# Sigmoid attention with a top-1 mixture of experts: gate products as bfloat16 parts, scatters and value loads moved

## The chip, the cores and the metric

The kernel runs on one core of a Trainium2 chip. The metric is the device time of one execution in microseconds (us). A profile of one execution stands beside three timed runs; engines are named as the profile names them: PE (TensorE matmul), PEld (its weight loads), DVE (VectorE), ACT (ScalarE), POOL (GpSimd) and SP (SyncE, which here only issues DMAs).

## The reference

Attention with a sigmoid in place of the softmax, over 8 batches, 12 heads, 448 positions and head size 64, gives a row of 768 numbers for each of 3584 tokens. Then each token goes to the one of 8 experts with the largest logit:

```python
scores = scale * np.matmul(q, k.transpose(0, 1, 3, 2)) - np.log(S)
x = np.matmul(1.0 / (1.0 + np.exp(-scores)), v)      # tokens x 768 after a transpose
logits = x @ w_gate
e = argmax(logits);  gate = softmax(logits)[e]
out[token] = gate * (relu(x @ w1[e]) @ w2[e])        # w1: 768x1024, w2: 1024x768
```

## The kernel before

**Attention.** A batch of 448 tokens is a block, 12 heads are 6 pairs of heads, and two pairs together are a unit of `ST` = 7 steps, one for each chunk of 64 key positions. A step `s` issues four score products (L612, recorded as 8 instructions), two sigmoids on ACT (L599), and the four products with the values of step `s - 2` (L627). `PB` = 21 steps are one block. Within a stretch of 21 steps a step is named below by its place r, 0 to 20. At the end of a unit ACT and DVE copy the sums out of PSUM (L635, L636) and DVE transposes them for a token-major copy in DRAM (L464), which SP writes (L472). Queries and keys arrive transposed in 32x32 blocks (`load_pair`, L519, eight DMAs for a pair) and DVE turns them (`turn`, L582). Values arrive by `load_values` (L526 for an even pair, one DMA; L570 for an odd one, two DMAs). The two PSUM tiles of a unit come from one of two pools; two following units that use the same pool share its two tiles.

**Routing.** For each block `gate_a` to `gate_d` compute the logits, the expert of each token, its gate, and where its record (row, gate) goes in a DRAM list `recs`; `put_records` scatters the records by four indirect DMAs on POOL (L417). The tiles `si` and `rec` that a scatter reads exist once.

**Dense stage.** A block's tokens are then all run through the expert that most of them chose (`moe`): 8 sums for the hidden layer of 18 products each (L249), then 6 sums of 24 (L268), 288 products in all, each operand split into a high and a low part. A product is one `yield`; a tick of the interleaving is 14 of them. The results are multiplied by the gates in a second layout, `gate_rows`: `gate_m` (L433) spreads the block's gates over 14 columns, and `gate_e` (L440, L442) brings them to the right partitions by four float32 products with the 0/1 matrix `place`, into a PSUM tile of the attention's pool, which DVE copies. Both are issued in the ticks 5 and 6 of the stage, those of the last block in ticks 8 and 9 of the stage before.

**Skipped stages.** For the blocks 1 to 5 (`LEFT`) the dense stage stands in an `If` on the flag that over 240 tokens chose the expert; the branch stands behind step r = 1 of the stretch two blocks later. Otherwise the `Else` only loads and turns what the steps to come need, and attention goes on. In this data one of the five, block 4, takes the `Else`. Its tokens, and those of the other experts, are run at the end from the records, gathered by row.

**Order.** The program's order on each engine is written out by hand under `tc.manual_schedule()`: dictionaries say at which step or tick a load, a turn or a gate step is issued (`LATER`, `LAST`, `BETWEEN`, `BESIDE_GATES`, `LATE_GATES`). Each DMA queue (SP's, POOL's) is in order. The letters in the `GATES` tables are the gate steps, "p" the scatter, "m" and "e" the two gate steps of the dense stage, "x" the token-major writes.

Of the kernel before, what the change touches and what calls it, by code (L numbers as in the profile page):

```python
# [25 lines left out]
def tile_sigmoid_attention_top1_moe(  # L26
# [86 lines left out]
    HR = 16  # L113
    place = const.tile([P, P + HR], F32, name="place")
    spot = const.tile([CP, NCH, NB], F32, name="spot")

    def places():

        aside = opool.tile([P, 512], F32, tag="ob", name="aside")
        halves = aside[:, : 2 * HR].rearrange("p (h r) -> p h r", h=2)  # L120
        nc.vector.tensor_reduce(
            halves, ident.rearrange("p (i h r) -> p h r i", i=4, h=2), axis=AX.X, op=ALU.add
        )
        for h in range(2):
            to = place.rearrange("p (n r) -> p n r", r=HR)[:, h::2]
            nc.vector.tensor_copy(to, halves[:, h].unsqueeze(1).broadcast_to([P, 5 - h, HR]))
        off = aside[:CP, P : P + NCH * NB].rearrange("p (c j) -> p c j", c=NCH)
        nc.gpsimd.iota(
            off, pattern=[[CP, NCH], [-32, NB]], base=0, channel_multiplier=1, allow_small_or_imprecise_dtypes=True
        )  # L130
        nc.vector.tensor_scalar(spot, off, 0.0, None, op0=ALU.is_ge)
        nc.vector.scalar_tensor_tensor(spot, off, 32.0, spot, op0=ALU.is_lt, op1=ALU.mult)

# [99 lines left out]
    def moe(b, wts):  # L233
# [7 lines left out]
        for j in range(KF):  # L241
# [3 lines left out]
            for t in range(KD):  # L245
                xh, xl = xch[b, t]
                ws = slice(t * P, (t + 1) * P)
                for n, (a, b_) in enumerate(((whi, xh), (whi, xl), (wlo, xh))):
                    nc.tensor.matmul(ps[:, :S], a[:, ws], b_, start=(t == 0 and n == 0), stop=(t == KD - 1 and n == 2))  # L249
                    yield  # L250
            if j % 2 == 0:
                two = [hpool.tile([P, 1024], F32R, tag=f"h{x}{j}", name=f"h{x}_{b}_{j}") for x in "hl"]
# [177 lines left out]
    def gate_m(b):  # L430

        gm[b] = small.tile([CP, NCH, NB], F32, tag="gm", name=f"gm_{b}")
        nc.vector.tensor_tensor(gm[b], spot, gates[:CP, b].unsqueeze(2).broadcast_to([CP, NCH, NB]), op=ALU.mult)  # L433

    def gate_e(b):

        pg = small_ps(b, "pg")
        by_place = gm.pop(b)
        for c in range(NCH):
            nc.tensor.matmul(pg[:, :NB], place[:CP, c % 2 * HR : c % 2 * HR + P], by_place[:, c], start=(c == 0), stop=(c == NCH - 1))  # L440
        gate_rows[b] = small.tile([P, NB], F32, tag="gt", bufs=2, name=f"gt_{b}")
        nc.vector.tensor_copy(gate_rows[b], pg[:, :NB])  # L442

# [172 lines left out]
    def weighted(s):  # L616
# [40 lines left out]
        0: lambda u: turn(2 * u + 2, "k"),  # L657
        1: lambda u: (turn(2 * u + 2, "q"), load_values(2 * u + 2)),
        3: lambda u: turn(2 * u + 3, "k"),
        4: lambda u: (turn(2 * u + 3, "q"), load_values(2 * u + 3)),  # L660
    }
# [38 lines left out]
    def attention():  # L700

        order = ExitStack()
        order.enter_context(tc.manual_schedule())
        for g in range(2):
# [16 lines left out]
        def gate_step(b, what):  # L721
# [13 lines left out]
            elif what == "m":  # L735
                gate_m(b)
            elif what == "e":
                gate_e(b)
            elif what == "x":
# [9 lines left out]
        BESIDE_GATES = {  # L749
            0: "xa", 1: "b", 3: "c", 4: "l", 6: "d", 7: "p", 8: "m", 9: "e", 11: (0,), 12: (1,), 13: (2,),  # L750
        }
# [3 lines left out]
        LATE_GATES = {  # L755
            2: "a", 4: "b", 6: (0, "c"), 7: (1,), 8: (2, "l"), 11: "d", 16: "p",
        }
        ALONE = 2 * PB

        for s in range(N_ST + 2):  # L760
# [25 lines left out]
            for what in LATE_GATES.get(r, ()) if late else ():  # L786
                gate_step(nb, what)
            if i in (1, 5) and not ALONE - ST < s < ALONE + 2 or s == ALONE - 5:
                gate_step(None, "x")
# [10 lines left out]
            if b in LEFT:  # L800
# [10 lines left out]
                with tc.If(whole >= 1, label=f"whole_{b}") as whole_if, tc.manual_schedule():  # L811
                    for tick in range(14):
                        if tick in (5, 6):
                            gate_step(b, "me"[tick - 5])
                        if tick == 0:
# [6 lines left out]
                with whole_if.Else(), tc.manual_schedule():  # L822
# [4 lines left out]
                    load_values(2 * u + 3)  # L827
                    load_pair(2 * u + 4)
                    for at in rows:
                        token_rows(*at)  # L830
                    load_pair(2 * u + 5)
                    for g in (6, 7):
                        load_pair(2 * u + g, nc.gpsimd)
                continue
            for tick in range(0 if b else 1, 20 if b < B - 2 else 15):
                yield TICK
                for what in (BESIDE_GATES if b else FIRST_GATES).get(tick, ()):
                    gate_step(b + 1, what)
                if tick in (5, 6):
                    gate_step(b, "me"[tick - 5])  # L840
                if b == 0 and tick == 2:
                    put_records(0)
                todo = BETWEEN if b else FIRST_BETWEEN
# [4 lines left out]
            if b == 0:  # L848
                for n in range(2):
                    scores(ALONE + n)  # L850
        order.close()

# [17 lines left out]
    def until(n):  # L870
        more(left - n)

    for n in attention():
        more(n)
    att.close()


    order = ExitStack()
    order.enter_context(tc.manual_schedule())
    rest = ctx.enter_context(tc.tile_pool(name="rest", bufs=1))  # L880
# [335 lines left out]
```

## Time and profile before

| | us |
|---|---|
| three timed runs: median (lowest to highest) | 787.92 (785.06 to 789.79) |
| the profiled execution: its own time | 788.64 |
| the profiled execution: its span | 786.9 |
| PE busy | 772.8 (98%), granted clock 0.994 of full speed |
| DVE busy, ACT busy, POOL busy | 439.3, 374.7, 140.9 |
| gate products L440: 56 instructions, busy | 6.7 |

Busy time on PE is that of pipelined instructions, so a busy stretch is compared by the starts of its instructions. Times in the rows are us from the start of the span.

### The profile page before, as it was taken

The page shows a single profiled execution, that of the slowest core. Times are in us where ns is not written, and L with a number is a line of the kernel's source. Part 1 is how long each engine was busy: PE and PEld are TensorE (multiplying, and loading weights), DVE is VectorE, ACT ScalarE, POOL GpSimd, SP SyncE. Part 2 cuts the span into 40 slices and gives each one's busy share as a digit, 9 for nine tenths or more (in the row PEclk, how much of TensorE's full clock was granted, in tenths as well). Part 3 has the DMA queues.
Part 4 walks back from the last instruction along what each step waited for, and adds up shares of the span by engine and source line. Part 5 has one row for each costly group of instructions (what it writes and reads, how often), then busy time and mean ns, then how long its engine had stood idle before and what let it go on. Part 6 is the DMA issues. An engine that isn't in the chain of part 4 may idle for free. (4 is left out here: it accounts for less than half of the span.)

```text
span 786.9 us, 15431 instructions
## 1 busy us (share of the span) xinstructions
PE 772.8 (98%) x5536; PEld 592.3 (75%) x5536; DVE 439.3 (56%) x944; ACT 374.7 (48%) x681; POOL 140.9 (18%) x217
## 2 busy tenths in 40 slices
PE   9999999999999999999999969999999999999996
PEld 5545899789974699647996424799648998999885
DVE  3465767335437754376443837654376574476763
ACT  5876432863217632284323838532383321435662
POOL 4433204100021001210012151001220232031011
PEclk9999999999999999999999989999999999999999
DMA  8968789557524984268932586981266356599111
GB/s 170 187 131 219 177 199 222 106 113 189 105 53 101 237 208 95 48 145 216 213 58 46 79 178 149 238 197 24 47 161 176 101 130 173 185 295 320 53 36 38
DMA packets 268147, 114.45 MB, mean 145 GB/s; under 512 B 192380, under 2 KB 257932, under 8 KB 268062
## 3 DMA queue, kind: packets, MB, share of 16 engines
q1 hardware_dynamic: 258766, 91.82, 48.9%
q0 software_dynamic: 8864, 20.87, 11.1%
q8 instruction: 46, 0.75, 0.4%
q10 hardware_dynamic: 432, 0.69, 0.3%
q14 instruction: 39, 0.32, 0.2%
HBM read 94.30 MB, written 22.38 MB: 148 GB/s over the span
## 5 line engine op out<-in xcount | busy, mean ns | idle before, releaser
L599 ACT ACTIVATE at<-sc,bias_s 128x448 f32<-128x448 f32 x336 | 195.2, 634 | 127.1 <-PE sc L612 125.7
L627 PE MATMUL av<-at,vn 64*64 64x448 f32 x1344 | 184.1, 538 | 5.9 <-DMA vn<-in_v_dram 4.9
L612 PE MATMUL sc<-qt,kt 64*64 64x448 f32 x1344 | 184.6, 545 | 0.2 <-PEq L811 0.2
L612 PEld LDWEIGHTS sc<-qt,kt 64*64 64x64 f32 x1344 | 83.2, 189 | 58.6 <-issue 41.3
L249 PE MATMUL ps<-xh,w1h 128*128 128x448 f32 x336 | 124.4, 370 | 0.0
L249 PE MATMUL ps<-xh,w1l 128*128 128x448 f32 x336 | 123.7, 368 | 0.0
L268 PE MATMUL ps<-hh,w2h 128*128 128x448 f32 x336 | 123.0, 366 | 0.0
L249 PE MATMUL ps<-xl,w1h 128*128 128x448 f32 x336 | 123.0, 366 | 0.0
L268 PE MATMUL ps<-hh,w2l 128*128 128x448 f32 x336 | 123.0, 366 | 0.0
L268 PE MATMUL ps<-hl,w2h 128*128 128x448 f32 x336 | 122.8, 365 | 0.0
L284 POOL DMA_DIRECT2D out_dram<-ob x84 | 53.8, 647 | 359.6 <-DVE ob L279 353.8
L627 PEld LDWEIGHTS av<-at,vn 64*64 64x64 f32 x1344 | 63.7, 133 | 65.3 <-issue 61.3
L254 ACT ACTIVATE hh<-ps 128x448 fp32r<-128x448 f32 x56 | 30.5, 545 | 145.3 <-PE ps L249 145.3
L177 ACT CAST w2h<-wst 128x512 fp32r<-128x512 f32 x84 | 54.1, 662 | 81.1 <-PE ps L268 79.4
L178 DVE TENSOR_TENSOR w2l<-wst,w2h 128x512 fp32r<-128x512 f32 x84 | 56.7, 688 | 54.1 <-ACT w2h L177 52.2
L255 DVE SCALAR_TENSOR_TENSOR hl<-ps,hh 128x448 fp32r<-128x448 f32 x56 | 34.9, 622 | 76.2 <-ACT hh L254 76.1
L249 PEld LDWEIGHTS ps<-xh,w1h 128*128 128x128 f32 x336 | 63.1, 188 | 9.0 <-issue 3.5
L249 PEld LDWEIGHTS ps<-xh,w1l 128*128 128x128 f32 x336 | 63.1, 188 | 6.8 <-issue 1.1
L249 PEld LDWEIGHTS ps<-xl,w1h 128*128 128x128 f32 x336 | 63.1, 188 | 5.8 <-issue 0.4
L268 PEld LDWEIGHTS ps<-hh,w2h 128*128 128x128 f32 x336 | 63.1, 188 | 5.1 <-issue 0.2
L268 PEld LDWEIGHTS ps<-hl,w2h 128*128 128x128 f32 x336 | 63.1, 188 | 4.9
L268 PEld LDWEIGHTS ps<-hh,w2l 128*128 128x128 f32 x336 | 63.1, 188 | 4.9
(154 smaller groups left out, 821.7 us busy)
## 6 DMA issues: line engine op xcount, KB each, us to landing
wst<-in_moe_w_dram SPq DMA_DIRECT2D x50, 512.0 KB, 3.9
wst<-in_moe_w_dram SPq DMA_DIRECT2D x56, 384.0 KB, 5.3
x_tok<-xt SPq DMA_DIRECT2D x64, 168.0 KB, 2.8
kn<-in_k_dram SPq DMA_DIRECT2D x176, 56.0 KB, 3.7
out_dram<-ob POOLq DMA_DIRECT2D x84, 112.0 KB, 3.0
qn<-in_q_dram SPq DMA_DIRECT2D x160, 56.0 KB, 2.9
kept<-in_moe_w_dram SPq DMA_DIRECT2D x12, 512.0 KB, 9.5
vn<-in_v_dram SPq DMA_DIRECT2D x16, 224.0 KB, 4.9
```

What stands on the lines that cost most here:

```text
L177: (nc.vector.tensor_copy if early else nc.scalar.copy)(hi, st)
L178: eng.tensor_tensor(lo, st, hi.bitcast(F32), op=ALU.subtract)
L249: nc.tensor.matmul(ps[:, :S], a[:, ws], b_, start=(t == 0 and n == 0), stop=(t == KD - 1 and n == 2))
L254: nc.scalar.activation(hh[:, :S], ps[:, :S], AF.Relu)
L255: nc.vector.scalar_tensor_tensor(hl[:, :S], ps[:, :S], 0.0, hh[:, :S].bitcast(F32), op0=ALU.max, op1=ALU.subtract)
L268: nc.tensor.matmul(ps[:, :S], a, b_, start=(j == 0 and n == 0), stop=(j == KF - 1 and n == 2))
L284: nc.gpsimd.dma_start(out[b * S : (b + 1) * S, cols].rearrange("(j r) f -> r j f", r=32), obv[32 * i : 32 * (i + 1)])
L599: nc.scalar.activation(at, ps[:, :S], AF.Sigmoid, bias=bias_s, scale=SCALE)
L612: nc.tensor.matmul(ps[quarter(g, h), :S], ks, ops[g, "q"][OWN[h]], start=True, stop=True)
L627: nc.tensor.matmul(psv[g][OWN[h], :S], ops[g, "v"][rows, c, :], at[rows], start=(c == 0), stop=(c == KC - 1))
```

## The change

- The gates are split by DVE into three bfloat16 parts whose sum is the float32 gate (`gate_m`: four small operations ahead of the product, which grows from 56 to 168 columns), `place` and `spot` become bfloat16, and the four float32 products become two bfloat16 products of 42 columns.
- These two products are issued behind the last product of the sixth hidden sum (j = 5), into the 64 columns of that PSUM bank that the sum leaves free; a DVE reduction adds the three parts in place of the copy. Step "e" goes from the tables, "m" stays at tick 5 (tick 8 for the last block).
- The scatter of a late stretch, issued at r = 16, is issued at r = 10 of the next late stretch, just ahead of the gate step "d" of r = 11; the last such one at tick 2 of the stage of block 6.
- In `LATER` the values of both pairs of the next unit are loaded in step 1; those of the odd pair were loaded in step 4.
- In the `Else` the second pair's loads go from SP to POOL and the third pair's from POOL to SP.
- The scope of the manual order is opened ahead of the attention and stays open into the last section.

```diff
-    place = const.tile([P, P + HR], F32, name="place")
-    spot = const.tile([CP, NCH, NB], F32, name="spot")
+    HB = NB // 2
+    place = const.tile([P, P + HR], BF16, name="place")
+    spot = const.tile([CP, NCH, HB], BF16, name="spot")
...
+            if j == 5:
+                gate_e(b, ps[:, S : S + 3 * NB])
...
     def gate_m(b):
-        gm[b] = small.tile([CP, NCH, NB], F32, tag="gm", name=f"gm_{b}")
-        nc.vector.tensor_tensor(gm[b], spot, gates[:CP, b].unsqueeze(2).broadcast_to([CP, NCH, NB]), op=ALU.mult)
-    def gate_e(b):
-        pg = small_ps(b, "pg")
+        ga = gates[:CP, b].rearrange("p (h n) -> p n h", n=2)
+        parts = small.tile([CP, 3, 2, 2], BF16, tag="parts", name=f"parts_{b}")
+        rem = small.tile([CP, 2, 2], F32, tag="rem", name=f"rem_{b}")
+        nc.vector.tensor_copy(parts[:, 0], ga)
+        nc.vector.tensor_sub(rem, ga, parts[:, 0])
+        nc.vector.tensor_copy(parts[:, 1], rem)
+        nc.vector.tensor_sub(parts[:, 2], rem, parts[:, 1])
+        gm[b] = small.tile([CP, 3, NCH, HB], BF16, tag="gm", name=f"gm_{b}")
+        sh = [CP, 3, NCH, HB]
+        nc.vector.tensor_tensor(
+            gm[b], spot.unsqueeze(1).broadcast_to(sh),
+            parts.rearrange("p k n h -> p k (n h)").unsqueeze(3).broadcast_to(sh), op=ALU.mult,
+        )
+    def gate_e(b, pg):
         by_place = gm.pop(b)
-        for c in range(NCH):
-            nc.tensor.matmul(pg[:, :NB], place[:CP, c % 2 * HR : c % 2 * HR + P], by_place[:, c], start=(c == 0), stop=(c == NCH - 1))
+        pgv = pg.rearrange("p (k j) -> p k j", k=3)
+        for n in range(2):
+            at = by_place[:, :, 2 * n : 2 * n + 2].rearrange("p k h j -> p k (h j)")
+            nc.tensor.matmul(pgv, place[:CP, n * HR : n * HR + P], at, start=(n == 0), stop=(n == 1))
         gate_rows[b] = small.tile([P, NB], F32, tag="gt", bufs=2, name=f"gt_{b}")
-        nc.vector.tensor_copy(gate_rows[b], pg[:, :NB])
+        nc.vector.tensor_reduce(gate_rows[b], pgv.rearrange("p k j -> p j k"), axis=AX.X, op=ALU.add)
...
     LATER = {
-        1: lambda u: (turn(2 * u + 2, "q"), load_values(2 * u + 2)),
+        1: lambda u: (turn(2 * u + 2, "q"), load_values(2 * u + 2), load_values(2 * u + 3)),
         3: lambda u: turn(2 * u + 3, "k"),
-        4: lambda u: (turn(2 * u + 3, "q"), load_values(2 * u + 3)),
+        4: lambda u: turn(2 * u + 3, "q"),
...
         LATE_GATES = {
-            2: "a", 4: "b", 6: (0, "c"), 7: (1,), 8: (2, "l"), 11: "d", 16: "p",
+            2: "a", 4: "b", 6: (0, "c"), 7: (1,), 8: (2, "l"), 11: "d",
...
+            if late and r == 10:
+                for last in list(ranked):
+                    put_records(last)
...
                     load_pair(2 * u + 4)
+                    load_pair(2 * u + 5, nc.gpsimd)
                     for at in rows:
                         token_rows(*at)
-                    load_pair(2 * u + 5)
-                    for g in (6, 7):
-                        load_pair(2 * u + g, nc.gpsimd)
+                    load_pair(2 * u + 6)
+                    load_pair(2 * u + 7, nc.gpsimd)
...
-                if b == 0 and tick == 2:
-                    put_records(0)
+                if tick == 2:
+                    for last in list(ranked):
+                        put_records(last)
```

## Rows read from the trace of the kernel before

**Rows 1.** Busy time of each engine by stretch: length, then PE first; PEclk near the end.

```profile
230.80:265.40 34.60, 34.60 (x366) 16.39 (x365) 24.12 (x67) 25.43 (x48) 6.53 (x9) 1.00 0.55 120
...
464.00:466.00 2.00, 2.00 (x17) 0.79 (x20) 0.00 (x0) 0.00 (x0) 2.00 (x4) 0.50 1.09 304
```

**Rows 2.** Waits of PE over the whole span: total us, times, longest.

```profile
PE av L627 <- DMA vn<-in_v_dram: 4.9, 1, 4.9
```

**Rows 3.** Timeline of PE around the skipped stage: start, us, instruction, [idle before].

```profile
454.40 1.04 PE L612 MATMUL sc<-qt,kt 64*64 64x448 f32 x8 [0.21 <-PEq L811]
456.43 0.97 PE L627 MATMUL av<-at,vn 64*64 64x448 f32 x4 [0.99 <-PE sc L612]
462.26 2.35 PE L627 MATMUL av<-at,vn 64*64 64x448 f32 x4 [4.87 <-DMA vn<-in_v_dram]
...
466.89 1.04 PE L612 MATMUL sc<-qt,kt 64*64 64x448 f32 x8
```

**Rows 4.** Timeline of SP's queue around the skipped stage.

```profile
443.69 0.37 SPq L526 DMA_DIRECT2D vn<-in_v_dram  x1
...
458.91 1.12 SPq L570 DMA_DIRECT2D vn<-in_v_dram  x2
...
465.20 1.13 SPq L570 DMA_DIRECT2D vn<-in_v_dram  x2
466.51 2.02 SPq L519 DMA_DIRECT2D kn<-in_k_dram  x4
```

**Rows 5.** All DMAs of line L570: time from issue to landing.

```profile
DMA to landing us min/median/max: 2.4/3.9/5.9
```

**Rows 6.** Timeline of DVE: an ordinary stretch, then the skipped stage.

```profile
346.55 0.17 DVE L405 TENSOR_SCALAR si<-sl 112x4 uint32<-112x4 f32 x1
...
456.76 0.63 DVE L464 STREAM_TRANSPOSE xt<-av 128x448 f32<-128x448 f32 x1
...
477.32 0.65 DVE L582 STREAM_TRANSPOSE kt<-kn 128x448 f32<-128x448 f32 x1
...
483.21 0.60 DVE L582 STREAM_TRANSPOSE qt<-qn 128x448 f32<-128x448 f32 x1
```

**Rows 7.** Timeline of PE: an ordinary step r = 2, then two steps after the skip.

```profile
231.67 0.93 PE L627 MATMUL av<-at,vn 64*64 64x448 f32 x8
...
233.81 1.04 PE L612 MATMUL sc<-qt,kt 64*64 64x448 f32 x8
...
477.27 0.93 PE L612 MATMUL sc<-qt,kt 64*64 64x448 f32 x8
...
484.79 0.93 PE L612 MATMUL sc<-qt,kt 64*64 64x448 f32 x8
```

**Rows 8.** Timeline of PE around the gate products of block 0.

```profile
97.28 0.37 PE L249 MATMUL ps<-xl,w1h 128*128 128x448 f32 x1
97.48 0.96 PE L440 MATMUL pg<-gm,place 112*128 112x14 f32 x8
...
98.58 0.37 PE L249 MATMUL ps<-xh,w1h 128*128 128x448 f32 x1
```

**Rows 9.** Timeline of PE around two bfloat16 products (`gate_c`) in the same stage.

```profile
91.42 0.36 PE L249 MATMUL ps<-xh,w1h 128*128 128x448 f32 x1
91.63 0.19 PE L355 MATMUL pc<-oh,ones 112*128 112x32 bf16 x1
...
91.98 0.37 PE L249 MATMUL ps<-xh,w1l 128*128 128x448 f32 x1
```

**Rows 10.** Timeline of DVE and of PE: `gate_m` of block 0, start of its seventh sum.

```profile
96.31 0.21 DVE L433 TENSOR_TENSOR gm<-spot,gates 112x56 f32<-112x56 f32 x1
...
100.41 0.37 PE L249 MATMUL ps<-xh,w1h 128*128 128x448 f32 x1
```

**Rows 11.** Timeline of POOL at the end of an ordinary dense stage.

```profile
327.22 2.50 POOL L284 DMA_DIRECT2D out_dram<-ob  x4 [6.51 <-DVE ob L279]
...
351.47 0.94 POOL L417 DMA_INDIRECT recs<-rec,si  x1 [0.30 <-issue]
```

**Rows 12.** All scatters of line L417: time from issue to landing.

```profile
DMA to landing us min/median/max: 2.1/4.9/10.1
```

More of the change, by code (lines that the diff above doesn't have):

```diff
@@ L126, in places @@
             nc.vector.tensor_copy(to, halves[:, h].unsqueeze(1).broadcast_to([P, 5 - h, HR]))
[L127 to L132, printed above, removed]
+        off, ge = (aside[:CP, n * P : n * P + NCH * HB].rearrange("p (c j) -> p c j", c=NCH) for n in (1, 2))
+        for n in range(2):
+            nc.gpsimd.iota(
+                off[:, 2 * n : 2 * n + 2], pattern=[[0, 2], [-32, HB]], base=n * CP, channel_multiplier=1,
+                allow_small_or_imprecise_dtypes=True,
+            )
+        nc.vector.tensor_scalar(ge, off, 0.0, None, op0=ALU.is_ge)
+        nc.vector.scalar_tensor_tensor(spot, off, 32.0, ge, op0=ALU.is_lt, op1=ALU.mult)
     wgp = const.tile([P, KD, GC], F32, name="wgp")
@@ L430, in gate_m @@
     def gate_m(b):
-        gm[b] = small.tile([CP, NCH, NB], F32, tag="gm", name=f"gm_{b}")
-        nc.vector.tensor_tensor(gm[b], spot, gates[:CP, b].unsqueeze(2).broadcast_to([CP, NCH, NB]), op=ALU.mult)
-    def gate_e(b):
-        pg = small_ps(b, "pg")
+        ga = gates[:CP, b].rearrange("p (h n) -> p n h", n=2)
[10 more added lines that the diff above has]
+            parts.rearrange("p k n h -> p k (n h)").unsqueeze(3).broadcast_to(sh), op=ALU.mult,
+        )
+    def gate_e(b, pg):
         by_place = gm.pop(b)
-        for c in range(NCH):
-            nc.tensor.matmul(pg[:, :NB], place[:CP, c % 2 * HR : c % 2 * HR + P], by_place[:, c], start=(c == 0), stop=(c == NCH - 1))
+        pgv = pg.rearrange("p (k j) -> p k j", k=3)
+        for n in range(2):
+            at = by_place[:, :, 2 * n : 2 * n + 2].rearrange("p k h j -> p k (h j)")
+            nc.tensor.matmul(pgv, place[:CP, n * HR : n * HR + P], at, start=(n == 0), stop=(n == 1))
         gate_rows[b] = small.tile([P, NB], F32, tag="gt", bufs=2, name=f"gt_{b}")
-        nc.vector.tensor_copy(gate_rows[b], pg[:, :NB])
+        nc.vector.tensor_reduce(gate_rows[b], pgv.rearrange("p k j -> p j k"), axis=AX.X, op=ALU.add)
     def load_regs(b):
@@ L700, in attention @@
     def attention():
-        order = ExitStack()
-        order.enter_context(tc.manual_schedule())
         for g in range(2):
@@ L736, in gate_step @@
                 gate_m(b)
-            elif what == "e":
-                gate_e(b)
             elif what == "x":
@@ L749, in attention @@
         BESIDE_GATES = {
-            0: "xa", 1: "b", 3: "c", 4: "l", 6: "d", 7: "p", 8: "m", 9: "e", 11: (0,), 12: (1,), 13: (2,),
+            0: "xa", 1: "b", 3: "c", 4: "l", 6: "d", 7: "p", 8: "m", 11: (0,), 12: (1,), 13: (2,),
         }
@@ L812, in attention @@
                     for tick in range(14):
-                        if tick in (5, 6):
-                            gate_step(b, "me"[tick - 5])
+                        if tick == 5:
+                            gate_step(b, "m")
                         if tick == 0:
@@ L838, in attention @@
                     gate_step(b + 1, what)
-                if tick in (5, 6):
-                    gate_step(b, "me"[tick - 5])
-                if b == 0 and tick == 2:
-                    put_records(0)
+                if tick == 5 and b < B - 1:
+                    gate_step(b, "m")
+                if tick == 2:
+                    for last in list(ranked):
+                        put_records(last)
                 todo = BETWEEN if b else FIRST_BETWEEN
@@ L850, in attention @@
                     scores(ALONE + n)
-        order.close()
     wts = Weights([(lambda b=b: regs.get(b)) for b in range(B)])
@@ L871, in until @@
         more(left - n)
+    order = ExitStack()
+    order.enter_context(tc.manual_schedule())
     for n in attention():
@@ L875, in tile_sigmoid_attention_top1_moe @@
     att.close()
-    order = ExitStack()
-    order.enter_context(tc.manual_schedule())
     rest = ctx.enter_context(tc.tile_pool(name="rest", bufs=1))
```

## Prediction, made before the change was run

> **What bounds the kernel now.** I read the busy times by stretch first. In an ordinary attention stretch PE is busy for all of its length at the full granted clock, and the next engine, ACT, for 25.4 of its 34.6 us [rows 1]; the dense stages look the same. So only work taken off PE, or a stop of PE, can move the end. The list of PE's waits then shows that there is one stop worth the name: 4.9 us, once, for a load of values [rows 2]. The timeline of PE shows where: at the skipped stage of block 4. The scores of step r = 2 start at 454.40. Four of the eight value products start at 456.43, after 0.99 us of idling; the other four only at 462.26, after 4.87 us, and the next scores at 466.89 [rows 3]. In that stop PE's granted clock falls to 0.50, which is 1.2 GHz of 2.4 GHz [rows 1], and the four products take 2.35 us instead of 0.97 [rows 3]. The reader should see two losses there: the stop, and the slow time behind it.
>
> SP's queue shows why. The even pair's values were issued at 443.69, the odd pair's at 458.91, over 15 us later [rows 4]: between the two stand the loads of another pair and the token-major writes, which the order puts between steps 1 and 4. In the ordinary stretches the dense stage stands in this place and covers the same lateness.
>
> **The change: the value load.** In the new order the odd pair's two DMAs follow the even pair's directly, so they are issued near 445. Even at the longest landing of such a load, 5.9 us [rows 5], the data are there by 451, ahead of 457. What is late next? This unit and the one before it share their two PSUM tiles, and DVE's last transpose out of them ends at 456.76 + 0.63 = 457.39 [rows 6]. So the second four products start near 457.5. From the start of the value products to the next scores an ordinary step r = 2, the logits between them, takes 233.81 - 231.67 = 2.14 us [rows 7]; four products are half a step's value products, 0.37 us, already done, so 1.77 remain and the next scores come at 459.3. Against 466.89 that is 7.6 us: 4.76 of the stop, 2.86 of the slow clock. The 0.99 us before 456.43 stay; I take it that the clock does not fall for them, since it was at 1.0 after them in the trace until the long stop. If it falls all the same, up to 2.86 come back.
>
> Then everything after it on PE comes 7.6 us earlier, but SP's queue does not, since it issues its DMAs one behind another, whatever PE does. Two things get close. First, the next unit's values are issued at 465.20 to 466.33 [rows 4] and land after 3.9 us, 470.2, or 5.9 at the longest, 472.2. Their products started 0.75 us behind the scores of 477.27 [rows 7], now 470.4: a stop of 0 to 1.8 us, and by the median none. Second, the keys of the pair after that are issued until 468.53 [rows 4]. With 2.4 to 3.9 us to land, by the row of the nearest loads, they are there at 470.9 to 472.4. Between the turn of these keys and the end of the last turn of that unit DVE worked from 477.32 to 483.81, 6.5 us [rows 6], so the last turn ends at 477.4 to 478.9. PE's scores of that unit were at 484.79 [rows 7], now 477.2. That is a stop of 0.2 to 1.7 us; I take 1.0. So the skip gives 7.6 - 1.0 = **6.6 us**.
>
> The exchange in the `Else` sends one pair from SP to POOL and one back, eight DMAs each. The pair that goes to POOL comes earlier than it did, the other takes its place on SP, and the count on SP is the same: nothing. The Trainium skill ("DMA: Bandwidth & Descriptors", section "Issuing engines are not separate DMA queues") says that the DMAs of all issuing engines run on the same 16 engines, and that another issuer saves only issue time. Elsewhere both values are loaded 1.1 us of SP time ahead, and what stood there, the loads of a later pair, comes 1.1 us later; the pair's turn is needed only when the next unit's scores come, several steps on. If that cover were gone it would cost the 1.1 us.
>
> **The gate products.** In the dense stage of block 0 the products before and behind the gate products start at 97.28 and 98.58, one more standing between them: 1.30 us [rows 8]. Nearest to the new form are the two bfloat16 products of `gate_c` in the same stage: 112 rows, 128 weight columns, 32 moving columns against 42. There the same span is 91.98 - 91.42 = 0.56 us [rows 9]. I take that, and ten more columns as nothing: 0.74 us for each of the seven dense stages that run, **5.2 us**. The other bound: only the count is halved and a product costs as before; then half of 0.96 us [rows 8] is saved less the edges, about 0.4, 2.9 us in all.
>
> DVE gets four more operations of at most 0.21 us each and a product of 168 columns instead of 56, at most 0.63, so `gate_m` ends some 1.3 us later, plus gaps, at about 98. It is needed when the sixth sum ends, 100.41 less the 0.9 us that no longer stand ahead of it: 99.5 [rows 10]. The work queued behind it on DVE, the low halves of a hidden sum and of weights, comes 1.3 us later; the sixth sum still has to wait for neither. The reduction replaces the copy at the same size. The sum's own ReLU may have to wait for the two products behind it, about 0.15 us, while the next use of its bank is a whole sum away.
>
> **The scatters.** POOL loses nothing and gains nothing that PE waits for: no wait of PE ends on POOL. At r = 10 a scatter follows the last output writes of a dense stage in POOL's queue, and needs nothing new, so POOL issues it at once. In the stretch behind one stage the writes end at 327.22 + 2.50 = 329.7; four scatters of 0.94 + 0.30 us [rows 11] end at 334.7 and land by 339.6, or by 344.8 at the longest landing of 10.1 us [rows 12]. Behind them waits DVE's write of `si` at 346.55 [rows 6], because the scatter reads the only copy of it. So nothing waits. The order's wider scope changes no work: nothing.
>
> **The sum**, against the profiled execution's own 788.64 us: 788.64 - 6.6 - 5.2 = 776.8. That execution lies 0.7 us above the median of the three runs, so I predict **776.1 us** for a median.
>
> **The rivals.**
>
> *The stop moves down* (chance 0.18). All that I took as near comes true: the values of the next unit stop PE for up to 1.8 us, the turn for 1.7, or the clock falls for the 0.99 us and takes 2.86. For it: SP's queue is the same length and PE arrives 7.6 us earlier. Against: each lands in time by its median. With about half of the 7.6 given back, 3.3 us remaining: 788.64 - 3.3 - 5.2 = 780.1, as a median 779.4.
>
> *The values come late all the same* (0.09). If the 16 engines and not the queue's order set the landing, the odd pair's values land where they did, and only the gates pay: 783.4, as a median 782.7. Against: the even pair, issued at 443.69 on the same queue, stopped nobody at 456.43. The section of the Trainium skill named above is the rule that would make it so; the trace has no landing on that line longer than 5.9 us [rows 5].
>
> *The gates do not pay* (0.06). `gate_m` comes late for the sixth sum, PE waits in each stage what it saved. The spare is 1.5 us in block 0 [rows 10]; from 0.74 us beyond it nothing is left in that stage. Then 788.64 - 6.6 = 782.0, as a median 781.3. Against: it needs DVE to be over 2 us later than its operations add up to.
>
> *Slower* (0.04). DVE, in order, stops at `si` for the landing of the scatter just issued, in four stretches. The turns behind it are for scores ten steps later, 15 us at 1.5 us a step, of which I leave 5 for DVE's lag behind PE. So a landing is free up to about 346.55 + 10 = 356.5, where the longest seen would give 344.8 [rows 6, 12]. From 3 us past that in each of the four stretches the 11.8 us are eaten; with 5 us past it the time is 776.1 + 20 = 796.
>
> *It does nothing* (0.03): the order written out does not come out as the order on the queues, and the products cost what they did; 788.
>
> **How the numbers follow.** The likeliest case, both gains at about their size, has 0.60. About 0.5% (4 us, 784.0) is what a measurement here can tell from no change. Faster by more: 0.60 + 0.18 + 0.06 and half of the 0.09, which lies at the bound: 0.885. Within it: the other half and the 0.03: 0.075. Slower: 0.04. The range begins with both gains whole, 12.8 us, so 775.1, less the 2.9 us by which the lowest of the three runs lies below their median: about 772.5. It ends with the gates at 2.9 and the skip at 3.3 us: 781.7, and with some spread 782.5. Late values, the slower case and no change lie outside, under 0.2 together.
>
> **What the new profile would show.** Right: no wait of PE for values; the second four products at r = 2 of the skip near 457.5 less what the stages before saved (some 3.7 us); the granted clock at 1.0 through it; 0.56 us around two products of L440's successor behind the sixth sum; the write of `si` with no stop before it. Wrong: a new stop of PE within ten steps of the skip, longer than 1.7 us, or a half clock there; a wait of PE for `gm`; a spacing near 0.9 us around the gate products. The prediction falls if SP's queue, earlier by PE's time than I think, holds the loads of the steps behind the skip.

## The result, and the profile after

The changed kernel took 776.09 us, the median of four runs (774.96 to 777.61); the kernel before took 787.38 us in the same comparison (four runs, 785.06 to 789.79). The ratio is 0.9858, with a 95% interval of 0.9822 to 0.9894: faster by 1.4%, 11.3 us. The prediction was 776.1, its range 772.5 to 782.5. The profiled execution after took 774.96 us, with a span of 773.3.

PE's list of waits no longer holds the wait for values of [rows 2]. Each line gives engine, line, what it waited for, the total in us, the number and the longest:

```profile
PE av L644 <- PE sc L629: 1.0, 1, 1.0
PE ps_warm L607 <- PEq L1218: 0.9, 1, 0.9
PE sc L629 <- DVE qt L599: 0.6, 1, 0.6
```

The timeline of PE at the skipped stage, which answers to [rows 3]:

```profile
450.76 1.04 PE L629 MATMUL sc<-qt,kt 64*64 64x448 f32 x8 [0.21 <-PEq L827]
452.79 2.03 PE L644 MATMUL av<-at,vn 64*64 64x448 f32 x8 [0.99 <-PE sc L629]
454.75 1.34 PE L307 MATMUL psg<-x,wgp 128*32 128x224 f32 x24
456.02 1.04 PE L629 MATMUL sc<-qt,kt 64*64 64x448 f32 x8
```

All eight value products now stand in one line; they take 2.03 us where an undisturbed eight take 0.93, because the second four start at 453.85: 1.06 us behind the first, where an ordinary step has 0.38, so 0.7 us late. From the step's scores to the next scores it is 456.02 - 450.76 = 5.26 us, where it was 12.49. No half clock stands in this place: the granted clock is 1.00 until 769 us. SP's queue ([rows 4] before) shows the odd pair's two DMAs (L587) right behind the even pair's:

```profile
440.06 0.37 SPq L543 DMA_DIRECT2D vn<-in_v_dram  x1
440.53 1.49 SPq L587 DMA_DIRECT2D vn<-in_v_dram  x2
442.13 2.26 SPq L536 DMA_DIRECT2D kn<-in_k_dram  x4
444.49 1.98 SPq L536 DMA_DIRECT2D qn<-in_q_dram  x4
446.57 2.85 SPq L489 DMA_DIRECT2D x_tok<-xt  x4
```

The gate products in the dense stage of block 0, which answer to [rows 8] (the timeline of PE; the two gate products are L457):

```profile
99.88 0.37 PE L252 MATMUL ps<-xh,w1l 128*128 128x448 f32 x1
100.08 0.22 PE L457 MATMUL ps<-gm,place 112*128 112x42 bf16 x2
100.15 0.45 PE L252 MATMUL ps<-xh,w1h 128*128 128x448 f32 x1
100.44 0.37 PE L252 MATMUL ps<-xl,w1h 128*128 128x448 f32 x1
```

The span from the product before to the second one behind is 100.44 - 99.88 = 0.56 us; it was 1.30.

Where the rest of the time came from is read by setting the starts of the score products of all 168 attention steps of the two traces side by side. The span fell by 13.6 us:

| where | before | after | gained |
|---|---|---|---|
| step r = 2 at the skipped stage | 12.49 | 5.26 | 7.2 |
| five steps with a dense stage in them, each | 61.30 to 64.94 | 0.73 to 0.75 less | 3.7 |
| last step with all that follows, two dense stages among it | 199.15 | 197.46 | 1.7 |
| step r = 4 of four late stretches, each | 2.28 | 1.97 | 1.2 |
| step r = 6 of one late stretch | 2.07 | 1.76 | 0.3 |
| start of the kernel (first scores 0.3 us earlier) and step r = 7 of the first stretch (1.50 before, 2.29 after) | | | -0.5 |

The first two terms were predicted and so was the third, but for 0.2 us; the two behind them were not. The new stop of about 1 us that the prediction put at the second unit behind the skip is not in this execution: its steps take 1.50 us like any other. It is in the other profiled execution of the same kernel (experiment 7).

### The profile page after: what moved, and what is told of

Its sections match the earlier page's. It is cut to its first block, busy times and chain, and to the rows that moved or that the text cites. A ratio compares the mean times of both kernels' runs of the same rounds, so it can differ in the third digit from the quotient of the medians.

```text
span 773.3 us, 15360 instructions
## 1 busy us (share of the span) xinstructions
PE 763.8 (99%) x5494; PEld 584.3 (76%) x5494; DVE 444.8 (58%) x972; ACT 374.6 (48%) x681; POOL 142.1 (18%) x218
## 5 line engine op out<-in xcount | busy, mean ns | idle before, releaser
L644 PE MATMUL av<-at,vn 64*64 64x448 f32 x1344 | 181.3, 537 | 1.1 <-PE sc L629 1.0
```

The lines of the kernel that those rows point to most:

```text
L644: nc.tensor.matmul(psv[g][OWN[h], :S], ops[g, "v"][rows, c, :], at[rows], start=(c == 0), stop=(c == KC - 1))
```

## The experiments

The kernels ran in three groups, the experiments 1 to 4, 5 to 7 and 8 to 10, each group on one chip, and each kernel is compared with runs of the kernel before in its own group. The groups are not alike: in the second the kernel before took 787 us, in the first and third 795 to 796. What may make part of the difference shows in experiment 2. The one trace of the kernel before comes from a chip where it took 787 us; steps of all groups are compared with it.

**1. The values alone.**

```diff
-        1: lambda u: (turn(2 * u + 2, "q"), load_values(2 * u + 2)),
+        1: lambda u: (turn(2 * u + 2, "q"), load_values(2 * u + 2), load_values(2 * u + 3)),
-        4: lambda u: (turn(2 * u + 3, "q"), load_values(2 * u + 3)),
+        4: lambda u: turn(2 * u + 3, "q"),
```

> The kernel before with one edit: both values in step 1. If the order of SP's queue alone made the stop at the skipped stage, the scores of r = 2 and of r = 3 there stand about 5.3 us apart instead of 12.5, PE waits for no values, and the time falls by 7.2 us, to about 780. If the exchange in the Else or the scatters' leaving POOL made it, nothing moves: 787. The dense stages stay at 59.70 us, and the step r = 4 of the late stretches at 2.28 us if the values have nothing to do with it.

Measured: 793.20 us beside 795.42, ratio 0.9973 (0.9949 to 0.9996). The stop went as expected, the step at the skip took 4.79 us, but the time fell by only 2.2 us. In its trace the steps r = 17 and 18 of the late stretches and the steps r = 1 that follow on them are 10.7 us longer together than in the trace of the kernel before. How many of these the kernel before has on this chip is not known, since it has no trace there.

**2. The gates alone**: of the change only the hunks of `places`, `gate_m`, `gate_e` and their calls.

```diff
-        pg = small_ps(b, "pg")
...
+            if j == 5:
+                gate_e(b, ps[:, S : S + 3 * NB])
```

> The kernel before with the gates in three bfloat16 parts and their products behind the sixth sum, nothing else. Expected: dense stages of 58.96 us instead of 59.70, so 7 x 0.74 = 5.2 us less, about 782; the stop at the skip whole, 12.5 us. The step r = 4 of four late stretches, 2.28 us before and 1.97 after the whole change, tells who owns it: 1.97 here if it is the PSUM tile that the gate products no longer take from the attention's pool (then some 1.2 us more, 781), 2.28 if it is the scatters or the order's scope.

Measured: 792.20 us beside 795.42, ratio 0.9973 (0.9948 to 0.9998). The products of the stages took the same 0.74 us less as in the changed kernel, step r = 4 took 1.97 us in every late stretch, and the stop stayed: PE waited 4.54 us for `vn`, the step took 11.53. The time fell by 3.2 us, where 5.2 to 6.4 were expected. The timeline of ACT, PE and POOL late in the first late stretch shows where such time goes; in the trace of the kernel before no step here is long:

```profile
254.51 0.53 ACT L652 CAST xh<-av 128x448 fp32r<-128x448 f32 x1 [0.50 <-PE sc L629]
257.47 2.21 ACT L616 ACTIVATE at<-sc,bias_s 128x448 f32<-128x448 f32 x4 [2.42 <-remote]
...
254.41 0.93 PE L629 MATMUL sc<-qt,kt 64*64 64x448 f32 x8
255.16 0.93 PE L644 MATMUL av<-at,vn 64*64 64x448 f32 x8
258.15 2.29 PE L629 MATMUL sc<-qt,kt 64*64 64x448 f32 x8 [2.06 <-ACT at L616]
...
254.22 0.94 POOL L422 DMA_INDIRECT recs<-rec,si  x1 [0.30 <-issue]
255.47 0.95 POOL L422 DMA_INDIRECT recs<-rec,si  x1 [0.30 <-issue]
```

The score products end at 254.41 + 0.93 = 255.34, and ACT, idle since 255.04, starts on them only at 257.47; the profile calls the releaser remote, that is, it finds none. The semaphore records have it: the signal of these products is stamped 257.38, 2.04 us after their end. PE waits for ACT to free a score tile, stands still from 256.09 to 258.15, and then its clock falls (the windows' columns: stretch, length, busy time and count of PE, PEld, DVE, ACT and POOL, granted clock, DMA share, GB/s):

```profile
255.00:259.00 4.00, 1.94 (x18) 0.79 (x14) 3.97 (x8) 1.58 (x4) 1.11 (x2) 0.91 1.21 285
259.00:262.00 3.00, 3.00 (x22) 1.81 (x18) 2.93 (x5) 1.83 (x4) 0.00 (x0) 0.55 1.44 165
```

I counted such signals in every trace. In the six from chips where the kernel before took 787 us (before, after and the second group), none of the some 700 signals of PE came over 0.3 us after the end of its products. In the eight of the other two groups some 30 in each did (a few records are missing, so the count is rough), by up to some 5 us, nearly all while POOL was issuing the indirect scatters or just behind. So these chips seem to differ in something that the profile does not name. It was not found out what.

**3. The changed kernel with the values as before.**

```diff
-        1: lambda u: (turn(2 * u + 2, "q"), load_values(2 * u + 2), load_values(2 * u + 3)),
+        1: lambda u: (turn(2 * u + 2, "q"), load_values(2 * u + 2)),
-        4: lambda u: turn(2 * u + 3, "q"),
+        4: lambda u: (turn(2 * u + 3, "q"), load_values(2 * u + 3)),
```

> The changed kernel with the odd pair's values back in step 4. If the queue's order is the cause, the stop for the values comes back, some 12 us from r = 2 to r = 3 at the skip, and the time is 776.1 + 7.2 = 783. If the emptier POOL queue or the Else's exchange cured it, the time stays at 776.

Measured: 785.32 us beside 795.42, ratio 0.9887 (0.9837 to 0.9937), and **no stop for values**: the step at the skip took 5.48 us. This is against the theory on which the prediction stood. The odd pair's values stood behind the same loads in SP's queue as before, and were issued at 451.66 instead of 458.91. Something that the change moves besides them had slowed the queue.

**4. The gate products in a tile of their own**, in tick 6 as before, in the new form:

```diff
-            if j == 5:
+            if j == 5 and b == B - 1:
...
+                if tick == 6:
+                    gate_e(b, small_ps(b, "pg")[:, : 3 * NB])
```

> The changed kernel with the bfloat16 products in a PSUM tile of their own from the attention's pool, in tick 6 as before (the last block's stay behind its sixth sum). If the price is in the float32 products alone, the dense stages stay at 58.96 us. If the tile in the attention's pool makes the slow step r = 4, that step goes back from 1.97 to 2.28 us in the four stretches, and the time rises by 1.2 us, to 777; if not, 776 and 1.97.

Measured: 783.66 us beside 795.42, ratio 0.9860 (0.9810 to 0.9909). The stages gain the same 0.74 us. Step r = 4 took 2.28 us again in all four stretches. So the bfloat16 form brings the gain in the stages, and the place in the spare columns brings the 0.31 us, which the prediction had not seen. Before, after and this kernel, the score products of that step in the third late stretch:

```profile
423.88 1.24 PE L612 MATMUL sc<-qt,kt 64*64 64x448 f32 x8
```

```profile
420.86 0.93 PE L629 MATMUL sc<-qt,kt 64*64 64x448 f32 x8
```

```profile
422.91 1.24 PE L629 MATMUL sc<-qt,kt 64*64 64x448 f32 x8
```

Where the gate products take a turn of the pool of score tiles, the eight products of this step stand 0.31 us further apart. How the turn does it was not tried.

**5. The scatters alone**, on the kernel before:

```diff
-            2: "a", 4: "b", 6: (0, "c"), 7: (1,), 8: (2, "l"), 11: "d", 16: "p",
+            2: "a", 4: "b", 6: (0, "c"), 7: (1,), 8: (2, "l"), 11: "d",
...
+            if late and r == 10:
+                for last in list(ranked):
+                    put_records(last)
```

> Only the record scatters are moved (to step 10 of the next stretch); gates, both value loads and the exchange of the pairs stay as before. Theory A (the values were late because the scatters' small packets hold the 16 DMA engines ahead of the skip): the stop for the odd values goes although their load is still issued in step 4, and the step behind the score products after the skip falls from 12.5 us to about 5.3; time about 7 us under the kernel before. Theory B (the values were late because they stood behind two pairs and the stores in the SP queue, or because of the exchange of the pairs, as the prediction had it): the step stays near 12 us and the time within 1 us of before. The gate steps stay at 1.30 us per stretch either way.

Measured: 787.61 us beside 787.23, ratio 1.0005 (0.9993 to 1.0017). Theory A's mechanism is there, and its time is not. The step at the skip took 5.27 us, with the values loaded where they were before. SP's queue, kernel by kernel, says why. The kernel before:

```profile
446.20 5.41 SPq L519 DMA_DIRECT2D qn<-in_q_dram  x4
451.84 6.05 SPq L472 DMA_DIRECT2D x_tok<-xt  x4
```

The scatters alone moved:

```profile
445.26 1.99 SPq L519 DMA_DIRECT2D qn<-in_q_dram  x4
447.34 2.23 SPq L472 DMA_DIRECT2D x_tok<-xt  x4
449.92 0.54 SPq L200 DMA_DIRECT2D wst<-in_moe_w_dram  x2
450.59 1.13 SPq L570 DMA_DIRECT2D vn<-in_v_dram  x2
```

The same eight DMAs (four each of L519 and L472) take 11.5 us to issue in one and 4.2 in the other. In the kernel before POOL issues the scatters from 442.19 to 446.96, and they land 9.6 us later in the median; the windows of these microseconds show engines that are busy and move little. Before, and with the scatters moved:

```profile
444.00:448.00 4.00, 4.00 (x49) 1.80 (x44) 3.38 (x7) 3.65 (x8) 2.35 (x3) 1.00 0.71 47
448.00:452.00 4.00, 4.00 (x48) 1.95 (x44) 3.90 (x7) 3.00 (x6) 0.00 (x0) 1.00 0.87 106
```

```profile
444.00:448.00 4.00, 4.00 (x48) 1.95 (x44) 3.97 (x8) 3.39 (x7) 0.00 (x0) 1.00 0.77 148
448.00:452.00 4.00, 4.00 (x48) 1.94 (x44) 3.79 (x6) 3.23 (x6) 0.00 (x0) 1.00 0.82 194
```

At about the same share the engines move 47 GB/s beside the scatters and 148 without. The scatters write 448 records of 8 bytes. The DMA engines are not busy with these: by the list of the queues in the kernel before from 444 to 452 us (packets, MB, share of the 16 engines' time; q1 is SP's queue, q0 POOL's) the time goes to SP's own packets.

```profile
q1 hardware_dynamic: 3112, 0.60, 75.2%
q0 software_dynamic: 94, 0.00, 0.8%
```

With the scatters moved, q1 has 5701 packets in a share of 79.3%. So an SP packet takes nearly twice as long in the mean (31 ns of engine time against 18) while scatters are out; by what way they slow it, no run shows.

Most of what the edit gains at the skip is lost 12 steps on: step r = 14 took 3.59 us and r = 16 took 4.32, 4.9 us above two ordinary ones, behind a wait of 1.9 us for DVE and one of 2.3 for `vn`; step r = 1 of the next stretch takes 0.7 us more. That is 5.6 of 7.2 us in the profiled execution, which is the fastest of the ten (785.56 us). Its mean granted clock is 0.999, that of the other nine 0.994 to 0.997; of this a fall at the very end of the kernel can take 0.003 (the first trace of the changed kernel has no other, and 0.997). So in most of the nine the clock fell in another place too, and that the rest of the gain goes there fits, but they have no trace.

**6. The changed kernel without the exchange of the pairs.**

```diff
-                    load_pair(2 * u + 5, nc.gpsimd)
                     for at in rows:
                         token_rows(*at)
-                    load_pair(2 * u + 6)
-                    load_pair(2 * u + 7, nc.gpsimd)
+                    load_pair(2 * u + 5)
+                    for g in (6, 7):
+                        load_pair(2 * u + g, nc.gpsimd)
```

> The changed kernel with the exchange of the two pairs between the SP and GpSimd queues undone. The prediction put this part at zero: same time as the changed kernel within 1 us, step behind the skip 5.3 us. If the exchange is what emptied the SP queue, the step goes back to 8 to 12 us and the time rises by 3 to 7 us.

Measured: 784.15 us beside 787.23, ratio 0.9954 (0.9934 to 0.9974), 8.7 us above the changed kernel in the same group (experiment 7). Step r = 2 at the skip stays at 5.26 us, so the exchange did not empty the queue for the values; the loss is again at the end of the second unit, where step r = 14 takes 9.33 us and the two behind it 2.99 and 1.94. The timelines of SP, POOL, DVE and PE give the chain:

```profile
465.38 4.03 SPq L536 DMA_DIRECT2D kn<-in_k_dram  x4
469.51 3.58 SPq L536 DMA_DIRECT2D qn<-in_q_dram  x4
...
465.85 0.99 POOL L422 DMA_INDIRECT recs<-rec,si  x1 [0.77 <-issue]
...
475.84 0.65 DVE L599 STREAM_TRANSPOSE kt<-kn 128x448 f32<-128x448 f32 x1 [2.46 <-DMA kn<-in_k_dram]
480.24 0.65 DVE L599 STREAM_TRANSPOSE qt<-qn 128x448 f32<-128x448 f32 x1 [3.75 <-DMA qn<-in_q_dram]
...
481.03 1.02 PE L629 MATMUL sc<-qt,kt 64*64 64x448 f32 x2 [6.85 <-DVE pre L399]
```

The moved scatters are now under way from 465.85 on, and the pair that SP loads in the same microseconds lands only near 480, by DVE's waits for it. Without the exchange that pair is the next one to be turned. DVE stands at it for 3.75 us, and PE for 6.85. The windows show the second loss behind it, as at the old stop: the granted clock is at 0.53 and 0.50, the level of 1.2 GHz.

```profile
472.00:476.00 4.00, 2.17 (x20) 0.70 (x12) 1.54 (x4) 2.22 (x4) 0.00 (x0) 1.00 1.05 61
476.00:480.00 4.00, 0.00 (x0) 0.00 (x0) 0.48 (x1) 0.00 (x0) 0.13 (x1) 0.53 0.75 186
480.00:484.00 4.00, 2.97 (x16) 1.13 (x20) 2.78 (x13) 0.63 (x1) 0.00 (x0) 0.50 0.78 165
```

With the exchange POOL issues that pair ahead of the scatters (455.62 to 460.62 in the changed kernel), and the one that SP loads beside them is wanted a unit later.

**7. The changed kernel again, and with the scatters put back** (experiment 5's edit, the other way).

> The changed kernel itself, unaltered, on the same chip as the other three, as their yardstick: ratio to the kernel before 0.985 to 0.987, step behind the skip 5.3 us, no wait for values. If the late signals during the indirect DMAs are a matter of the chip, they show in all four runs of this call or in none.

> The changed kernel with the scatters put back into step 16 and everything else as changed. If both edits remove the stop by themselves (values early or scatters late), no stop for values comes back, the step behind the skip stays at 5 to 6 us, and the time is that of the changed kernel on a chip where the scatters disturb nothing else, and 5 to 8 us above it where the signals of TensorE come late while the scatters are issued (2 to 4 us of lost steps at steps 17 to 19 of each late stretch). If the scatters are the only thing that matters, about 7 us come back at the skip.

Measured beside 787.23 us: the changed kernel 775.48, ratio 0.9850 (0.9822 to 0.9877); with the scatters back 776.89, ratio 0.9868 (0.9842 to 0.9893). The intervals overlap, and the profiled executions stand the other way round (spans of 774.1 and 773.3). Step r = 2 at the skip takes 5.27 and 5.26 us. So on this chip the scatters' new place is worth nothing that was measured, once the values are early; experiment 9 has another answer from a chip with late signals. All four traces of the second group are without late signals, where those of the other two groups all have them, of much the same kernels. It seems to go with the chip and not with the kernel, though no one kernel has a trace on both.

The trace of the changed kernel in this group has the new stop that the first one lacks, at step r = 14 behind the skip, by the chain that the prediction named: DVE waits 1.69 us for a pair's queries, its last turn of the unit ends at 474.14, and PE, which was there at 473.19, starts the second half of the step's products at 474.29.

```profile
471.37 0.65 DVE L599 STREAM_TRANSPOSE qt<-qn 128x448 f32<-128x448 f32 x1 [1.69 <-DMA qn<-in_q_dram]
473.54 0.60 DVE L599 STREAM_TRANSPOSE qt<-qn 128x448 f32<-128x448 f32 x1
...
473.19 0.92 PE L629 MATMUL sc<-qt,kt 64*64 64x448 f32 x4
474.29 0.65 PE L629 MATMUL sc<-qt,kt 64*64 64x448 f32 x2 [0.18 <-DVE pre L399]
```

Step r = 14 takes 1.91 us. From there the first and the last score product of a step start 1.2 us apart instead of 0.4, up to the next dense stage, and the step with that stage takes 61.35 us instead of 60.57. So the stop costs 1.2 us in all, of which the starts of the steps show 0.4 at once. With the scatters back that step takes 61.20 us, 0.6 more; in the experiments 5 and 6 it is 0.7 longer than in the traces without such a stop.

**8. Early values and gates, with neither the scatters nor the pairs moved; and the values alone again.** The first is the changed kernel with experiment 5's edit undone and experiment 6's made, the second has the edit of experiment 1.

> The changed kernel with both the scatters and the exchange of the pairs put back, so that only the early values, the gates and the scope of the order are left. Theory A (the exchange is needed only because the moved scatters hold the DMA engines while the second pair behind the skip is on its way): no stop at step 14 behind the skip, step behind the skip 5.3 us, time within 2 us of the changed kernel (775 to 777 us where before is 787). Theory B (the exchange is needed with or without the moved scatters): a stop of 4 to 9 us at steps 13 to 16 behind the skip, time 780 to 785 us.

> The kernel before with the odd unit's values loaded beside the even one's, and nothing else. If the signals of TensorE come in time on this chip: the step behind the skip falls from 12.5 to about 5.3 us, the pair behind it still comes in time because the scatters stay in their old place, and the time is 780 to 781 us where before is 787. If they come late again while the scatters are issued, 2 to 4 us of steps are lost in each late stretch, as in the first values-only run, and the gain is 2 to 4 us.

Measured beside 795.78 us: 788.86 (ratio 0.9911, 0.9890 to 0.9931) and 792.37 (0.9973, 0.9947 to 0.9999). By its ratio the first would speak for theory B (0.9911 of 787 us is 780). But the signals came late in both, so the steps have to speak. The step at the skip takes 4.79 and 4.80 us. Without the exchange, but with the scatters at r = 16, steps r = 13 and 14 lose 1.7 us, not 9.8: theory A, with a rest. The lost steps at r = 17 to 19 of the late stretches, which go with late signals, are there too, with 0.7 to 2.4 us in each, less than the 2 to 4 expected, and 0.5 to 0.8 us more in the step with the dense stage behind them.

**9. The scope of the order as before**, in the changed kernel.

```diff
     def attention():
+        order = ExitStack()
+        order.enter_context(tc.manual_schedule())
...
+        order.close()
```

> The changed kernel with the scope of the hand-written order as before (the stretch of attention inside, the last loop in a scope of its own). The prediction put this part at zero: the same time as the changed kernel within 1 us, and the same steps. If the scope lets the planner move work across the edge of the stretches, single steps at the skip or at the end differ by over 0.3 us.

Measured: 783.73 us beside 795.78, ratio 0.9853 (0.9825 to 0.9881). That is the changed kernel's ratio elsewhere, 0.9858 and 0.9850, and the step at the skip is 5.27 us. The changed kernel itself was not run in this group, so this compares chips; nothing that the scope is worth was found.

Beside experiment 8 in the same group, which has the scatters and the pairs in their old places, this is 5.1 us less (783.73 against 788.86, and the intervals of the two ratios do not meet). So on a chip with late signals the two moves together do bring time: in the traces the late stretches lose less with the scatters issued at r = 10, and the 1.7 us at r = 13 and 14 are not lost.

**10. The copies first**: the transposes for the token-major rows read the copies in SBUF.

```diff
-                token_block(g, pv[:, :S])
...
+            for g in two:
+                token_block(g, xch[divmod(g, NP)][1])
```

> The changed kernel with the copies out of the value products' PSUM tiles issued ahead of the token-major transposes, which then read the copies in SBUF. If the half step that TensorE loses between the two fours behind the skip is the wait for those PSUM tiles, the step falls from 5.26 to about 4.6 us and the time by 0.5 to 1 us below the changed kernel. If the transposes being later holds the queries' and keys' turns on VectorE, steps 3 to 5 grow instead and the time is the same or up to 2 us longer.

Measured: 782.71 us beside 795.78, ratio 0.9829 (0.9805 to 0.9853), 1.0 us below experiment 9 in the same group. The step at the skip is 4.13 us instead of 5.26, and the value products start closer behind their scores:

```profile
454.34 1.04 PE L629 MATMUL sc<-qt,kt 64*64 64x448 f32 x8 [0.20 <-PEq L828]
455.77 1.50 PE L644 MATMUL av<-at,vn 64*64 64x448 f32 x8 [0.39 <-DVE x L653]
```

So 1.1 us of what was left at the skip was the wait for the two PSUM tiles. That the time falls by it is not shown: 1.0 us is within the spread of these runs. Its ratio is the lowest of all, though the interval overlaps with those of the changed kernel; it was not run on a chip where the kernel before takes 787 us.

The cases at the skip together, from the starts of the score products (the last column is what steps r = 13 to 16 take above 1.50 us each; the 0.6 to 0.8 us that all four of the second group lose besides at the next dense stage, experiment 7, are not in it). The rows 2, 1, 8 and 3 are from chips with late signals:

| kernel | values | scatters | pairs | step r = 2 | lost behind |
|---|---|---|---|---|---|
| before | step 4 | old | old | 12.49 | 0 |
| 2 | step 4 | old | old | 11.53 | 0 |
| 1 | early | old | old | 4.79 | 0 |
| 8 (with gates) | early | old | old | 4.79 | 1.7 |
| 8 (values alone) | early | old | old | 4.80 | 0.2 |
| 5 | step 4 | moved | old | 5.27 | 4.9 |
| 3 | step 4 | moved | exchanged | 5.48 | 0.8 |
| 6 | early | moved | old | 5.26 | 9.8 |
| 7, scatters back | early | old | exchanged | 5.26 | 0 |
| changed (7) | early | moved | exchanged | 5.26 (5.27) | 0 (0.4) |

The stop is there only where neither the values nor the scatters were moved; either edit removes it. And a moved scatter costs 5 to 10 us unless the pairs are exchanged. Why three traces with early values have 4.79 or 4.80 us where the others have 5.26 is not known; in all three the scatters and the pairs are in their old places, and the signals come late.

## Why the prediction was right, and where it was not

**The time** was right, 776.1 against 776.09, and the two gains that it named carry the result. The likeliest case had a new stop of 1.0 us, which came in one of the two profiled executions of the changed kernel (1.2 us, experiment 7) and not in the other, and it missed the two small gains, 1.5 us; the two profiled executions differ by 13.7 us where the sum had 11.8, the medians by 11.3. A part of the fit is therefore luck of single executions.

**The skip**, 7.6 us: 7.2 measured. The predicted second four "near 457.5 less what the stages before saved (some 3.7 us)", so 453.8, start at 453.85, and they wait for DVE's hold on the PSUM tiles, as experiment 10 confirms. The missing 0.4 us is in the 1.77 that the prediction had from there to the next scores, which measured 456.02 - 453.85 = 2.17: it took off 0.37 us for four products already done, half of eight, but four take as long as eight (0.97 us [rows 3] against 0.93 [rows 7]). No low clock followed the 0.99 us of idling.

**Why the values were late**: wrong in half. The prediction had them wait for their place in SP's queue, between the pair and the token-major writes. The place mattered, since loading them earlier is enough (experiment 1). But the same place is no trouble when the scatters are elsewhere (3, 5): the queue was slow because scatters were under way beside it. The rival "the values come late all the same" named the right thing, the 16 engines that all queues share, and drew the wrong end from it: a transfer asked for in time gets through. The section of the Trainium skill that the prediction weighed there, "Issuing engines are not separate DMA queues" in "DMA: Bandwidth & Descriptors", says that DMAs interleave on the same engines whoever issues them. The trace agrees in this: beside POOL's scatters SP's eight issues took 11.5 us, without them 4.2. But the scatters' own packets had 0.8% of the engines' time (experiment 5), so the sharing as the prediction weighed it is not the price.

**The scatters at nothing**: right in sum on the chips of the second group, for a reason other than the one given. The prediction asked only whether POOL, `si` or PE would wait for them, and left out what they do to the DMAs beside them. Alone they take away one stop of 7.2 us and make another of 4.9; in the full change the second of these is 1.2 us or nothing (7). On a chip with late signals their move and the exchange together bring 5.1 us (9).

**The exchange at nothing**: this step failed. Counted as eight DMAs to each queue, it had no cost. In fact it decides which pair is loaded beside the moved scatters, and without it 8.7 us are lost. That is the rival "the stop moves down", at the place that the prediction gave for it, the turn at the end of the second unit, with 9.8 us where it was bounded by 1.7. The 1.7 rested on landings of 2.4 to 3.9 us [rows 5]; in experiment 6 the pair's queries, all issued by 473.09, were turned at 480.24, 7.2 us later.

**The gates**, 0.74 us a stage: right to 0.01 us in five stages. Of the last step's 1.7 us two stages explain 1.5; that step also differs by 0.5 us between the kernel before (199.15) and experiment 5 (198.65), where PE has the same work in both, so the 0.2 left are no sign of anything. The spare columns brought 1.2 us more at step r = 4 (experiment 4), a term that the sum lacked; the 0.3 us at r = 6 stays without a cause. PE has no wait for `gm`, and DVE idles at most 0.04 us before its writes of `si`. **The order's scope** at nothing: nothing else was found (9).

## What to carry to other kernels

A small transfer has to be costed by what it does to the transfers beside it, not by its bytes or by who waits for it: look for microseconds in which the DMA share is high and the GB/s are low, and at the issue times of the other queues there. When several edits are made together, a term put at zero may be what keeps another from costing; a table of on and off, as above, finds that in a few runs. And compare steps, not totals, when the total moves for reasons that lie outside the kernel.

## What the runs showed of the hardware

- Beside four indirect scatters of 112 records of 8 bytes the core's DMA moved 47 GB/s for 4 us, without them 148, at about the same busy share (0.71 and 0.77), and the issue of eight DMAs on another queue took 11.5 us instead of 4.2. The scatters' own packets took 0.8% of the engines' time (experiment 5).
- In two of three groups some of PE's signals came 0.3 to some 5 us late around such scatters, and a group of four cost up to some 4 us of steps; in the other group none did. The kernel before took 795 to 796 us in these two and 787 in the other. There is no trace of it from the slower two, so that late signals cost it the 8 us is argued, not shown, and why they come late is open.
- After stops of PE of 4.9 us [rows 1, 3] and 6.85 us (6) the granted clock stood at 0.50, and at 0.55 after one of 2.06 us (2). In the profiled execution of experiment 5, with stops of 1.9 and 2.3 us six microseconds apart, it stayed at 1.00; by the mean clock of the other nine executions (0.994 to 0.997 against its 0.999) it fell in most of them.
- Four value products that run without the other four take 0.97 us [rows 3], the eight together 0.93 [rows 7].
